# Transposes regrouped in the expert blocks, a relu shared with VectorE in 64-token blocks, and the first transposes of a fused attention + MoE kernel cut into parts

## The chip, the cores and the metric

The kernel runs on one core of one Trainium2 chip. The metric is the time of one execution on the device in microseconds (us), as the median of several executions. Three executions of the kernel before gave 520.6, 523.1 and 522.89 us: a median of 522.89. A profile comes from one further execution. Its engines are called PE (TensorE; PEld is its loading of the stationary operand), DVE (VectorE), ACT (ScalarE), POOL (GpSimd) and SP (SyncE, which here issues most DMAs).

## The reference

Sigmoid attention over 8 batches of 12 heads, 448 tokens and 64 dimensions; its rows are then tokens of a top-1 mixture of 8 experts, with a skip gate:

```python
scores = scale * np.matmul(q, k.transpose(0, 1, 3, 2)) - np.log(S)
attn = 1.0 / (1.0 + np.exp(-scores))
x = np.matmul(attn, v)                      # then reshaped to (3584, 768)
do_compute = x @ w_skip > 0
xc = x[do_compute]
e_idx = np.argmax(xc @ w_gate, axis=1)      # gate_w: its softmax weight
for e in range(8):
    mask = e_idx == e
    h = np.maximum(xc[mask] @ w1[e], 0.0)   # 768 -> 1024
    y[mask] = gate_w[mask, None] * (h @ w2[e])
out[do_compute] = xc + y
```

All inputs and outputs are float32.

## The kernel before

**Attention.** 48 steps, each a pair of heads of one batch. A step has four chunks `c` of keys. `prep` (L186) turns k and q of the pair with one VectorE block transpose each into a tile `x` whose partitions are the dimensions; `scores` (L197) makes a chunk's scores with four matmuls of 64x64 by 448 (224 in the last chunk); `weigh` (L227) takes the sigmoid on ACT; `values` (L231) multiplies by v, two chunks later, into `pa`; `keep_values` (L667) moves the result out of `pa` with one ACT copy (L668) and one VectorE add (L247). Before the first step, `keep_busy(10)` (L626) issues ten matmuls of the identity with itself; the first pair's k and q come in four small DMAs and are completed by copies on POOL and ACT (L607 to L609); the two transposes of the first pair are L627 and L628. All engines work through their instructions in the order in which this code is written (`tc.manual_schedule()`).

**Two blocks with the first expert.** After the last step, rows `x0` of 256 tokens, fetched by two gathers (L707), go through `turn_x` (L486: three 128x128 transposes on PE per half), `split_x` (L501: each float32 operand becomes a rounded part `xh` made by ACT, L495, and a rest `xl` made by DVE, L499), `gemm1` and `gemm2`. Their PSUM banks are those that attention's `pa` tiles had: three in a pool `ps_t` (through `new_t`) and one in `ps_b`. `b0_px0` and `b0_px1`, the turned rows of the first block, come from `new_t`; the one bank of `ps_b` is next used for the second half of the first block's hidden layer (`new_ph`, L799).

**The loop over the other blocks** (L1537). Each round picks one of four arms by a table that the kernel has made. In this run's order: one SPLIT, a HALF, a FULL, a HALF, then four times FULL and FEW, then a last FULL and FEW.

- FULL and SPLIT (`block`, L1323) work on 128 tokens: `gemm1(h)` makes half h of the hidden layer as 18 matmuls of 128x512 each, `relu` (ACT, L522), `turn_h(h)` (L524: four transposes into `pht[h]`), `split_h(h)` (L531: ACT makes `hh`, DVE makes `hl`), and `gemm2(j)` for j = 0..7, six matmuls of 128x384 each; j below 4 needs half 0, the others half 1. In between, the rows of the *next* block, `xn`, are turned into `pxt` (`turn_x`), after which `fetch` (L1266) lets POOL gather the rows of the block after that into `xn`, and `ready_x` (L1095) makes `xh`, `xf` (ACT) and `xl` (DVE) from `pxt`. SPLIT also splits the next expert's weights: the last statement of its arm (L1378) has DVE compute five rests of 128x768, `lo2(3)` to `lo2(7)` (L1224), after the block's own results are out.
- HALF (`half`, L1451) works on 64 tokens, with unsplit weights: two sides of 512 hidden columns land side by side in one PSUM bank, `ph[0]`; ACT applies relu in three pieces into `hs` (L1472); PE turns `xn` (6 transposes) and then `hs` (4 transposes, L1480) into the banks `pht[0]` and `ph[1]`; ACT copies them out in two pieces of 256 columns (L1486); then 32 matmuls make `py`. Its first instructions on DVE are the two of `take_rec` (L1315), which copy the block's record.
- FEW (`few`, L1382) does the same for 32 tokens.

Within an arm each engine follows the written order, and from round to round each engine passes from one arm straight to the next. The lines that set the order in HALF:

```python
for s in (slice(0, P), slice(P, 2 * P), parts[1]):
    nc.scalar.activation(hs[:, s], ph[0][:, s], AF.Relu)
...
for h in range(2):
    turn_x(xn, h, pxt[h])
fetch()
for c in range(4):
    nc.tensor.transpose(turned[c // 2][...], hs[:, c * P : (c + 1) * P], ident)
for s, p in zip(parts, turned):
    nc.scalar.activation(ht[:, s], p[:, : 2 * P], AF.Copy)
```

Of the kernel before, what the change touches and what calls it, by code (L numbers as in the profile page):

```python
# [10 lines left out]
F32 = mybir.dt.float32  # L11
# [3 lines left out]
AF = mybir.ActivationFunctionType  # L15
ALU = mybir.AluOpType
# [3 lines left out]
P = 128  # L20
# [3 lines left out]
def kernel(  # L24
# [11 lines left out]
    nc = tc.nc  # L36

    B, H, S, D = q.shape
# [4 lines left out]
    BT = 32  # L43
    NR7 = S // D
# [5 lines left out]
    NK2 = FF // P  # L50
# [23 lines left out]
    ident = const.tile([P, P], F32, name="ident")  # L74
# [43 lines left out]
    wk = att.enter_context(tc.tile_pool(name="wk", bufs=2))  # L118
# [8 lines left out]
    def new_s(name):  # L127

        turn[0] ^= 1
        return ps_s.tile([P, 2, 512], F32, tag=f"s{turn[0]}", name=name)  # L130
# [55 lines left out]
    def prep(b, hp, t, xs=None):  # L186

        n = 0 if xs is None else 1
        if xs is None:
            xs = wk.tile([P, 2, S], F32, tag="b0", name=f"x_{b}_{hp}")  # L190
        nc.vector.transpose(  # L191
            xs[:, n].rearrange("p (r j) -> p j r", j=NJ),
            t.rearrange("p (j d) -> p j d", d=D)[:, :, :BT],
        )
        return xs

    def scores(b, hp, c, xs):  # L197

        if (b, hp, c) == (0, 0, 2):
            sc = ps_a.tile([P, 2, 512], F32, tag="a", name="s_third")
        else:
            sc = new_s(f"s_{b}_{hp}_{c}")
        for m in range(2):
            first, qs = (4 * m + c, slice(0, S)) if c < 3 else (3, slice(m * HQ, (m + 1) * HQ))
            for j in range(2):
                r = slice(j * D, (j + 1) * D)
                nc.tensor.matmul(  # L209
                    sc[m * D : (m + 1) * D, j, : qs.stop - qs.start],  # L210
                    xs[r, 0, first::NR7],
                    xs[r, 1, qs],
                    start=True,
                    stop=True,
                )
        return sc
# [4 lines left out]
    def new_t(name):  # L221

        if ps_t is None:
            return new_s(name)[:, 0, :]
        return ps_t.tile([P, 512], F32, tag="t", name=name)
# [257 lines left out]
        nc.gpsimd.tensor_tensor(lo, r, hi, op=ALU.subtract)  # L483


    def turn_x(x, h, px):  # L486
        for j in range(3):
            i = 3 * h + j
            nc.tensor.transpose(  # L489
                px[:, j * P : (j + 1) * P], x[:, i * P : (i + 1) * P], ident  # L490
            )
# [29 lines left out]
    def relu(h, hs, ph):  # L521
        nc.scalar.activation(hs[:, h * H1 : (h + 1) * H1], ph[h], AF.Relu)  # L522

    def turn_h(h, hs, pt):  # L524
        for j in range(4):
            m = 4 * h + j
            nc.tensor.transpose(  # L527
                pt[:, j * P : (j + 1) * P], hs[:, m * P : (m + 1) * P], ident
            )
# [5 lines left out]
    def gemm2(j, hh, hl, py):  # L535
        h, m = divmod(j, 4)
        js = slice(m * P, (m + 1) * P)
        parts = [(n, o) for n in range(3) for o in range(2)]
        for n, o in parts:
            a, w = ((hh, wh2), (hh, wl2), (hl, wh2))[n]  # L540
            last = nc.tensor.matmul(  # L541
                half_y(py, o),
                a[h][:, js],
                w[j][:, o * H2 : (o + 1) * H2],
                start=(j == 0 and n == 0),
                stop=(j == NK2 - 1 and n == 2),
            )
        return last
# [33 lines left out]
    steps = [(b, hp) for b in range(B) for hp in range(NPAIR)]  # L582
# [33 lines left out]
    def part(n):  # L616
        return [kq[n // 2][:, j, n % 2] if n else kq0[:, j, 0] for j in range(2)]
# [4 lines left out]
    def keep_busy(n):  # L622
        for _ in range(n):
            nc.tensor.matmul(idle[:, 0, :P], ident, ident, start=True, stop=True)

    keep_busy(10)  # L626
    xs = prep(*steps[0], part(0)[0])  # L627
    xs = prep(*steps[0], part(0)[1], xs)  # L628
    ramp = const.tile([P, NX], F32, name="ramp")
    nc.vector.memset(ramp[:, NE:NX], 0.0)  # L630
    nc.vector.tensor_copy(ramp[:, :NE], ramp_i)
# [39 lines left out]
    for n, (b, hp) in enumerate(steps):  # L671
# [39 lines left out]
        for c in range(4):  # L711
            at = wk.tile([P, 2, S], F32, tag="A", name=f"at_{b}_{hp}_{c}", bufs=5)
            sc = scores(b, hp, c, xs)
# [71 lines left out]
        xs = xs_next  # L785
# [33 lines left out]
    for _ in range(2):  # L819
# [8 lines left out]
    ps_b = ctx.enter_context(  # L828
        tc.tile_pool(name="ps_b", bufs=1, space=bass.MemoryType.PSUM, reuse_waits="tile")
    )  # L830
    for h in range(2):
        px = new_t(f"b0_px{h}")
        turn_x(x0[0], h, px)
        split_x(h, px, xh0, xl0)
    logits(pl, [NK1 - 1], xt, 4)
# [2 lines left out]
    ph = new_ph(0)  # L838
    py = new_s("b0_py")
# [483 lines left out]
    def block(i, last):  # L1323


        def split1(js, h):
            if last:
                for j in js:
                    hi1(j, h)
                for j in js:  # L1330
                    lo1(j, h)

        look_ahead(ds(i + 3, 1))
        gemm1(0, range(G1), xh, xl, ph, last)
        relu(0, hs, ph)
        split1(range(3), 0)
        gemm1(1, range(9), xh, xl, ph, last)
        turn_h(0, hs, pht[0])
        split_h(0, pht[0], hh, hl)
        take_rec()  # L1340
        split1(range(3, NK1), 0)
        gemm1(1, range(9, G1), xh, xl, ph, last)
        relu(1, hs, ph)
        for h in range(2):
            turn_x(xn, h, pxt[h])
        fetch()
        split1(range(3), 1)
        gemm2(0, hh, hl, py)
        turn_h(1, hs, pht[1])
        split_h(1, pht[1], hh, hl)  # L1350
        split1(range(3, NK1), 1)
        if last:
            for h in range(2):
                whole_x(h, (slice(0, 3),))
        else:
            ready_x()
        next_rec(i)
        for j in range(1, NK2):
            gemm2(j, hh, hl, py)
        if last:  # L1360
            for j in range(2):
                hi2(j)
            for h in range(2):
                hi_x(h, pxt[h], xh)
            for j in range(2, NK2 - 2):
                hi2(j)
            for j in range(3):
                lo2(j)
            for j in range(NK2 - 2, NK2):
                dve.tensor_copy(wh2[j], raw2[j])  # L1370
            for h in range(2):
                lo_x(h, pxt[h], xh, xl)
        for o in range(2):
            rows = ys if last else yt
            weigh_sum(rows[:, o * H2 : (o + 1) * H2], half_y(py, o), recs[:, 0, 0:1])
        put(P, last)
        advance(1 if last else 2)
        if last:  # L1378
            for j in range(3, NK2):
                lo2(j)  # L1380
# [70 lines left out]
    def half(i):  # L1451

        nx = named()
        take_rec()

        def side(dst, g, n, a, w, j, most):
            nc.tensor.matmul(  # L1457
                dst[g * MD : (g + 1) * MD, :n],
                a,
                w,  # L1460
                start=(j == 0),
                stop=(j == most - 1),
                tile_position=(0, g * MD),
            )

        for j in range(NK1):
            for h in range(2):
                side(ph[0], h, H1, xf[:, j, :], raw1[j][h], j, NK1)
        turned = (pht[0], ph[1])
        parts = [slice(0, 2 * P), slice(2 * P, 4 * P)]  # L1470
        for s in (slice(0, P), slice(P, 2 * P), parts[1]):
            nc.scalar.activation(hs[:, s], ph[0][:, s], AF.Relu)  # L1472
        for h in range(2):
            for g in range(2):
                load_w1(g, h, nx)
        for h in range(2):
            turn_x(xn, h, pxt[h])
        fetch()
        for c in range(4):
            nc.tensor.transpose(  # L1480
                turned[c // 2][:, (c % 2) * P : (c % 2 + 1) * P],
                hs[:, c * P : (c + 1) * P],
                ident,
            )
        for s, p in zip(parts, turned):
            nc.scalar.activation(ht[:, s], p[:, : 2 * P], AF.Copy)  # L1486
        ready_x()

        ht8 = ht.rearrange("p (c h t) -> p c h t", c=4, h=2)
        for n in range(NK2):  # L1490
            c, h = divmod(n, 2)
            m = h * (NK2 // 2) + c
            for o in range(2):
                side(
                    py[1],
                    o,
                    H2,
                    ht8[:, c, h, :],
                    raw2[m][:, o * H2 : (o + 1) * H2],
                    n,  # L1500
                    NK2,
                )
        for g in range(3):
            load_w2(g, nx)
        look_ahead(ds(i + 3, 1))
        for o in range(2):
            s = slice(o * H2, (o + 1) * H2)
            weigh_sum(ys[:MD, s], py[1][o * MD : (o + 1) * MD, :H2], recs[:MD, 0, 0:1])
        next_rec(i)
        put(MD)  # L1510
        advance()
# [58 lines left out]
```

## Time and profile before

| what | value |
|---|---|
| median of 3 executions | 522.89 us (520.6 to 523.1) |
| the profiled execution: its time | 523.23 us |
| its span, from first to last instruction | 521.5 us |
| mean granted PE clock in it | 0.994 |
| attention | 0 to about 283 us |
| two blocks with the first expert | about 283 to 325 us |
| the loop's blocks | about 325 to 521.5 us |

The profiled execution took 1.7 us more than its span. A row of the timeline or of the chain of waits gives a start and a duration, both in us, then the engine, the line, the operation, output<-input and a count; in brackets stands how long the engine had been idle and what ended that. The chain of waits is followed back from the last instruction, at each step to what released it or, if nothing did, to the instruction before it on its engine. Rows of line groups give busy us and the mean ns of one.

### The profile page before, as it was taken

The page shows a single profiled execution, that of the slowest core. Times are in us where ns is not written, and L with a number is a line of the kernel's source. Part 1 is how long each engine was busy: PE and PEld are TensorE (multiplying, and loading weights), DVE is VectorE, ACT ScalarE, POOL GpSimd, SP SyncE. Part 2 cuts the span into 40 slices and gives each one's busy share as a digit, 9 for nine tenths or more (in the row PEclk, how much of TensorE's full clock was granted, in tenths as well). Part 3 has the DMA queues.
Part 4 walks back from the last instruction along what each step waited for, and adds up shares of the span by engine and source line. Part 5 has one row for each costly group of instructions (what it writes and reads, how often), then busy time and mean ns, then how long its engine had stood idle before and what let it go on. Part 6 is the DMA issues. An engine that isn't in the chain of part 4 may idle for free.

```text
span 521.5 us, 15403 instructions
## 1 busy us (share of the span) xinstructions
PE 506.7 (97%) x5031; PEld 343.2 (66%) x5032; DVE 292.4 (56%) x692; ACT 278.8 (53%) x481; POOL 239.5 (46%) x355
## 2 busy tenths in 40 slices
PE   8999999999999999999999999999999999999991
PEld 6885554555555555555445889857769797979790
DVE  3545766667668677776684872582221322349522
ACT  4776786766767866677666212661122323258321
POOL 3523454353556767665775401332331334444534
PEclk9999999999999999999999999999999999999997
DMA  8999977897999999999975105949395878797943
GB/s 206 201 233 194 198 159 153 178 178 171 197 195 239 216 194 205 215 193 224 199 158 111 26 31 163 386 131 356 116 339 214 251 300 283 269 328 234 346 185 47
DMA packets 142081, 107.22 MB, mean 206 GB/s; under 512 B 99163, under 2 KB 114523, under 8 KB 142032
## 3 DMA queue, kind: packets, MB, share of 16 engines
q1 hardware_dynamic: 133792, 96.11, 71.1%
q0 software_dynamic: 4032, 8.51, 6.8%
q10 hardware_dynamic: 4208, 1.95, 1.5%
q8 instruction: 30, 0.49, 0.4%
q14 instruction: 19, 0.16, 0.1%
HBM read 98.49 MB, written 17.56 MB: 223 GB/s over the span
## 4 chain that ended last, share of the span: by engine, by line
PE 91%; DMA 2%; DVE 2%; ACT 1%; issue 1%; POOL 1%; SPq 1%; ACTq 0%; POOLq 0%; DVEq 0%
PE s L209 24%; PE pa L237 23%; PE ph L513 11%; PE py L541 11%; PE b_ph L513 3%; PE b_py L541 3%; PE ph L1388 2%; PE py L1388 2%; PE py L1457 2%; PE ph L1457 2%; PE pxt L489 2%; PE pl L277 1%; PE pht L527 1%; DMA out_dram<-ys,rp 1%; PE pg L294 1%
## 5 line engine op out<-in xcount | busy, mean ns | idle before, releaser
L229 ACT ACTIVATE at<-s,bias 128x896 f32<-128x896 f32 (+1 forms) x191 | 173.5, 914 | 83.0 <-PE s L209 72.3
L209 PE MATMUL s<-x 64*64 64x448 f32 (+1 forms) x1528 | 172.3, 497 | 2.1 <-DVE sel L404 0.8
L237 PE MATMUL pa<-at,v 64*64 64x448 f32 (+1 forms) x1536 | 170.3, 489 | 0.0
L173 POOL COPY kq<-kq 32x896 f32<-32x896 f32 (+1 forms) x96 | 87.5, 912 | 97.6 <-DMA kq<-in_q_dram 48.7
L209 PEld LDWEIGHTS s<-x 64*64 64x64 f32 x1528 | 84.7, 191 | 51.2 <-issue 27.0
L237 PEld LDWEIGHTS pa<-at,v 64*64 64x64 f32 x1536 | 68.3, 133 | 54.1 <-issue 45.6
L191 DVE STREAM_TRANSPOSE x<-kq 128x448 f32<-128x448 f32 x94 | 80.7, 933 | 5.3 <-POOL kq L173 5.3
L247 DVE TENSOR_TENSOR xt<-xt,pa 128x448 f32<-128x448 f32 x48 | 29.8, 620 | 53.0 <-ACT xt L668 53.0
L411 POOL DMA_INDIRECT lst<-rec,idx x32 | 31.8, 995 | 16.7 <-issue 5.3
L483 POOL TENSOR_TENSOR wl<-wr,wh 128x384 fp32r<-128x384 f32 (+1 forms) x28 | 31.2, 1127 | 11.4 <-DVE wh L482 6.9
L252 DVE STREAM_TRANSPOSE y<-xt 128x448 f32<-128x448 f32 x48 | 31.0, 645 | 8.9 <-DMA out_dram<-y 7.4
L533 DVE TENSOR_TENSOR hl<-pht,hh 128x512 fp32r<-128x512 f32 x14 | 9.7, 690 | 41.8 <-ACT hh L532 35.1
L522 ACT ACTIVATE hs<-ph 128x512 f32<-128x512 f32 x14 | 8.4, 599 | 42.1 <-PE ph L513 26.2
L571 POOL DMA_INDIRECT out_dram<-ys,rp x15 | 22.8, 1520 | 16.2 <-POOLq L1537 8.4
L541 PE MATMUL py<-wh,hh 128*128 128x384 f32 x112 | 29.8, 347 | 0.0
L541 PE MATMUL py<-wh,hl 128*128 128x384 f32 x112 | 28.8, 338 | 0.0
L541 PE MATMUL py<-wl,hh 128*128 128x384 f32 x112 | 28.7, 337 | 0.0
L499 DVE TENSOR_TENSOR xl<-pxt,xh 128x384 fp32r<-128x384 f32 x30 | 15.3, 552 | 20.9 <-ACT xf L1087 20.2
L513 PE MATMUL ph<-wl,xh 128*128 128x512 f32 x84 | 26.3, 400 | 0.0
L668 ACT ACTIVATE xt<-pa 128x448 f32<-128x448 f32 x48 | 25.7, 536 | 0.8 <-PE pa L237 0.8
L513 PE MATMUL ph<-wh,xh 128*128 128x512 f32 x84 | 25.4, 399 | 0.0
L513 PE MATMUL ph<-wh,xl 128*128 128x512 f32 x84 | 24.1, 391 | 0.0
(263 smaller groups left out, 650.7 us busy)
## 6 DMA issues: line engine op xcount, KB each, us to landing
raw<-in_moe_w_dram SPq DMA_DIRECT2D x48, 768.0 KB
v<-in_v_dram SPq DMA_DIRECT2D x48, 256.0 KB
out_dram<-y SPq DMA_DIRECT2D x192, 56.0 KB
raw<-in_moe_w_dram SPq DMA_DIRECT2D x7, 1536.0 KB
kq<-in_k_dram SPq DMA_DIRECT2D x46, 224.0 KB
kq<-in_q_dram SPq DMA_DIRECT2D x46, 224.0 KB
wr<-in_moe_w_dram SPq DMA_DIRECT2D x12, 256.0 KB
wr<-in_moe_w_dram SPq DMA_DIRECT2D x16, 192.0 KB
```

The costliest lines, as they stand in the source:

```text
L173: nc.gpsimd.tensor_copy(a[BT:, :, :, :BT], a[:BT, :, :, BT:])
L191: nc.vector.transpose(xs[:, n].rearrange("p (r j) -> p j r", j=NJ), t.rearrange("p (j d) -> p j d", d=D)[:, :, :BT],)
L209: nc.tensor.matmul(sc[m * D : (m + 1) * D, j, : qs.stop - qs.start], xs[r, 0, first::NR7], xs[r, 1, qs], start=True, stop=True,)
L229: nc.scalar.activation(at[:, :, :n], sc[:, :, :n], AF.Sigmoid, bias=bias, scale=SCALE)
L237: nc.tensor.matmul(pa[j * D : (j + 1) * D, r, qs], vt[rs, j, r + c if c < 3 else 3 * (1 - r), :], at[rs, j, : qs.stop - qs.start], start=( ...
L247: nc.vector.tensor_tensor(x, x, pa[:, 1, :S], op=ALU.add)
L252: nc.vector.transpose(y, xts[b][:, hp, :])
L411: put = nc.gpsimd.indirect_dma_start(out=lst[:, :], out_offset=bass.IndirectOffsetOnAxis(ap=idx[:, c : c + 1], axis=0), in_=rec[:, c, :], ...
L483: nc.gpsimd.tensor_tensor(lo, r, hi, op=ALU.subtract)
L513: nc.tensor.matmul(ph[h], a[:, j * P : (j + 1) * P], w[j][h], start=(n == 0), stop=(n == len(t) - 1),)
L541: last = nc.tensor.matmul(half_y(py, o), a[h][:, js], w[j][:, o * H2 : (o + 1) * H2], start=(j == 0 and n == 0), stop=(j == NK2 - 1 and n ...
L668: nc.scalar.activation(xts[b][:, hp, :], pa[:, 0, :S], AF.Copy)
```

## The change

Four places. In HALF the second relu piece goes to VectorE, the last two pieces stay one ACT instruction, the first two pieces of `hs` are turned ahead of the last transpose of `xn`, and the copies out of PSUM are four of 128 columns. In `block`, `turn_x(xn)` and `fetch` go from before `gemm2(0)` to behind `turn_h(1)`, which itself now follows `gemm2(1)`. For the first pair, k is turned in four parts by chunk and q in two halves, between k's second and third part; the first chunk's scores are made by halves of the queries, and there are nine `keep_busy` matmuls instead of ten. `b0_px0` lies in `ps_b`'s bank.

```diff
@@ scores @@
+        if (b, hp, c) == (0, 0, 0):
+            by_u = [t.rearrange("p s (r u n) -> p s u r n", r=BT, u=2) for t in (xs, sc[:, :, :S])]
+            for u in range(2):
+                for m in range(2):
+                    for j in range(2):
+                        r = slice(j * D, (j + 1) * D)
+                        nc.tensor.matmul(
+                            by_u[1][m * D : (m + 1) * D, j, u],
+                            xs[r, 0, 4 * m :: NR7],
+                            by_u[0][r, 1, u],
+                            start=True,
+                            stop=True,
+                        )
+            return sc
@@ before the first step @@
-    keep_busy(10)
-    xs = prep(*steps[0], part(0)[0])
-    xs = prep(*steps[0], part(0)[1], xs)
+    keep_busy(9)
+    xs = wk.tile([P, 2, S], F32, tag="b0", name="x_first")
+    xv = xs.rearrange("p s (r u n) -> p s u n r", r=BT, u=2)
+    kv, qv = (t.rearrange("p (u n d) -> p u n d", u=2, d=D)[:, :, :, :BT] for t in part(0))
+    for c in range(4):
+        cs = slice(c, c + 5, 4) if c < 3 else slice(3, 4)
+        nc.vector.transpose(xv[:, 0, :, cs], kv[:, :, cs])
+        if c == 1:
+            for u in range(2):
+                nc.vector.transpose(xv[:, 1, u], qv[:, u])
@@ first block with the first expert @@
-        px = new_t(f"b0_px{h}")
+        px = new_t("b0_px1") if h else ps_b.tile([P, 512], F32, tag="b", name="b0_px0")
@@ block @@
         relu(1, hs, ph)
+        split1(range(3), 1)
+        for j in range(2):
+            gemm2(j, hh, hl, py)
+        turn_h(1, hs, pht[1])
         for h in range(2):
             turn_x(xn, h, pxt[h])
         fetch()
-        split1(range(3), 1)
-        gemm2(0, hh, hl, py)
-        turn_h(1, hs, pht[1])
         split_h(1, pht[1], hh, hl)
...
-        for j in range(1, NK2):
+        for j in range(2, NK2):
             gemm2(j, hh, hl, py)
@@ half @@
-        parts = [slice(0, 2 * P), slice(2 * P, 4 * P)]
-        for s in (slice(0, P), slice(P, 2 * P), parts[1]):
-            nc.scalar.activation(hs[:, s], ph[0][:, s], AF.Relu)
+        parts = [slice(c * P, (c + 1) * P) for c in range(4)]
+        nc.scalar.activation(hs[:, parts[0]], ph[0][:, parts[0]], AF.Relu)
+        nc.vector.tensor_scalar(hs[:, parts[1]], ph[0][:, parts[1]], 0.0, None, op0=ALU.max)
+        nc.scalar.activation(hs[:, 2 * P : 4 * P], ph[0][:, 2 * P : 4 * P], AF.Relu)
...
-        for h in range(2):
-            turn_x(xn, h, pxt[h])
+        def turned_h(cs):
+            for c in cs:
+                nc.tensor.transpose(turned[c // 2][:, parts[c % 2]], hs[:, parts[c]], ident)
+
+        turn_x(xn, 0, pxt[0])
+        turn_x(xn, 1, pxt[1], range(2))
+        turned_h(range(2))
+        turn_x(xn, 1, pxt[1], range(2, 3))
         fetch()
-        for c in range(4):
-            nc.tensor.transpose(
...
-        for s, p in zip(parts, turned):
-            nc.scalar.activation(ht[:, s], p[:, : 2 * P], AF.Copy)
+        turned_h(range(2, 4))
+        for c, s in enumerate(parts):
+            nc.scalar.activation(ht[:, s], turned[c // 2][:, parts[c % 2]], AF.Copy)
```

(`turn_x` gets a fourth argument, the transposes to do.) Where the change moves instructions, three places of the program, with the change's own line numbers in its rows. First PE in HALF, from the last matmuls into `ph` to the first into `py`; before:

```order
L489 MATMUL pxt<-ident,xn 128x128 x6
L1480 REGISTER_ALU
L1480 MATMUL pht<-ident,hs 128x128
L1480 REGISTER_ALU
L1480 MATMUL pht<-ident,hs 128x128
L1480 REGISTER_ALU
L1480 MATMUL ph_4385<-ident,hs 128x128 x2
L1457 ISA
L1457 MATMUL py_4387<-raw_0_4380,ht 64x384 x2
```

and of the change:

```order
L503 MATMUL pxt<-ident,xn 128x128 x5
L1502 REGISTER_ALU
L1502 MATMUL pht<-ident,hs 128x128
L1502 REGISTER_ALU
L1502 MATMUL pht<-ident,hs 128x128
L503 MATMUL pxt<-ident,xn 128x128
L1502 REGISTER_ALU
L1502 MATMUL ph_4392<-ident,hs 128x128 x2
L1479 REGISTER_ALU
L1479 MATMUL py_4394<-raw_0_4387,ht 64x384 x2
```

The second transpose of `hs`, which reads VectorE's piece, now stands ahead of the sixth of `xn`. Second, DVE and ACT around that relu, of the change, with the semaphores each row waits for. On DVE, the end of SPLIT's arm is five `wl` rows of L1245, and HALF's arm begins:

```order
L1338 COPY recs<-rn 128x2 [waits DMAHW0_I-4477_own,DVE_I-4477_own,DMAHW4_I-4477_own,DMAHW1_49]
L1339 REGISTER_ALU
L1339 CAST rid<-recs 128x1 [waits Pool_I-4477_own,DVE_I-4477_own,DMASW3_49,DVE_49]
L1494 REGISTER_ALU
L1494 TENSOR_SCALAR hs<-ph_4391 128x128 [waits Activation_I-4477_own]
L513 ISA
```

and on ACT the three pieces' rows and the copies stand as:

```order
L1493 ACTIVATE hs<-ph_4391 128x128 [waits PE_I-4477_own,Activation_I-4477_own,DVE_I-4477_own,Activation_49]
L1495 REGISTER_ALU
L1495 ACTIVATE hs<-ph_4391 128x256 [waits DVE_I-4477_own]
L1511 REGISTER_ALU
L1511 ACTIVATE ht<-pht 128x128 [waits PE_I-4477_own]
L1511 REGISTER_ALU
L1511 ACTIVATE ht<-pht 128x128 [waits Activation_I-4477_own]
```

VectorE's piece is the third instruction of DVE's arm; it waits on ACT (the first piece), and ACT's third piece waits on DVE: the three pieces, all read from the one bank `ph[0]`, are held one behind the other. Third, PE in FULL from the end of `gemm1(1)`; before:

```order
L489 MATMUL pxt<-ident,xn 128x128 x6
L541 ISA
L541 MATMUL py_4386<-wh_0_113,hh_4364 128x384
L541 REGISTER_ALU
L541 MATMUL py_4387<-wh_0_113,hh_4364 128x384
L541 MATMUL py_4386<-wl_0_121,hh_4364 128x384
L541 MATMUL py_4387<-wl_0_121,hh_4364 128x384
L541 REGISTER_ALU
L541 MATMUL py_4386<-wh_0_113,hl_4367 128x384
L541 MATMUL py_4387<-wh_0_113,hl_4367 128x384
L527 REGISTER_ALU
L527 MATMUL pht<-ident,hs 128x128 x4
```

and of the change, from the second half of `gemm2(0)` on:

```order
L555 MATMUL py_4393<-wh_0_113,hl_4374 128x384
L555 MATMUL py_4394<-wh_0_113,hl_4374 128x384
L555 MATMUL py_4393<-wh_1_114,hh_4371 128x384
L555 MATMUL py_4394<-wh_1_114,hh_4371 128x384
L555 MATMUL py_4393<-wl_1_122,hh_4371 128x384
L555 MATMUL py_4394<-wl_1_122,hh_4371 128x384
L555 MATMUL py_4393<-wh_1_114,hl_4374 128x384
L555 MATMUL py_4394<-wh_1_114,hl_4374 128x384
L541 REGISTER_ALU
L541 MATMUL pht<-ident,hs 128x128 x4
L503 MATMUL pxt<-ident,xn 128x128 x6
```

The ten transposes stand together behind twelve `py` matmuls, where before six of them stood ahead of the first `py` matmul and four behind the sixth.

More of the change, by code (lines that the diff above doesn't have):

```diff
@@ L483, in wsplit, with turn_x @@
         nc.gpsimd.tensor_tensor(lo, r, hi, op=ALU.subtract)
-    def turn_x(x, h, px):
-        for j in range(3):
+    def turn_x(x, h, px, js=range(3)):
+        for j in js:
             i = 3 * h + j
@@ L1475, in half @@
                 load_w1(g, h, nx)
-        for h in range(2):
-            turn_x(xn, h, pxt[h])
-        fetch()
-        for c in range(4):
[L1480 to L1484, printed above, removed]
-        for s, p in zip(parts, turned):
-            nc.scalar.activation(ht[:, s], p[:, : 2 * P], AF.Copy)
+        def turned_h(cs):
[5 more added lines that the diff above has]
+        turn_x(xn, 1, pxt[1], range(2, 3))
+        fetch()
+        turned_h(range(2, 4))
+        for c, s in enumerate(parts):
+            nc.scalar.activation(ht[:, s], turned[c // 2][:, parts[c % 2]], AF.Copy)
         ready_x()
```

## The prediction, made before the change was run

> **What bounds the kernel now.** I read the page first (span, busy shares, the shares of the chain of waits):
>
> ```profile
> span 521.5 us, 15403 instructions
> PE 506.7 (97%) x5031; PEld 343.2 (66%) x5032; DVE 292.4 (56%) x692; ACT 278.8 (53%) x481; POOL 239.5 (46%) x355
> PE 91%; DMA 2%; DVE 2%; ACT 1%; issue 1%; POOL 1%; SPq 1%; ACTq 0%; POOLq 0%; DVEq 0%
> ```
>
> PE is busy for 97% of the span and carries 91% of the chain. So only two things count: how long PE's own work takes, and the few places where it waits. What another engine gains or loses counts where PE waits for it. The chain of waits through the two HALF blocks and the FULL behind them (start, us, what) shows which places those are:
>
> ```profile
> 343.13 5.30 PE ph L1457 x24
> 348.43 0.81 PE pxt L489 x6
> 349.23 0.23 PE pht L1480 x2
> 349.47 0.02 issue
> 349.49 0.39 ACT ht L1486
> 349.88 0.09 issue
> 349.97 5.38 PE py L1457 x32
> ...
> 380.13 0.39 ACT ht L1486
> 380.53 0.09 issue
> 380.62 5.38 PE py L1457 x32
> ...
> 394.88 0.66 PE pxt L489 x6
> 395.53 1.05 PE py L541 x6
> 396.58 0.44 PE pht L527 x4
> 397.02 7.37 PE py L541 x42
> 404.39 2.76 PE ph L1388 x96
> 407.15 0.26 PE pht L1409
> 407.40 0.66 PE pxt L489 x6
> ```
>
> A HALF leaves the chain to ACT for about 0.5 us: PE has turned half of `hs` and waits for the first copy `ht` (0.39 + 0.09). In FULL and FEW the chain stays on PE. The sum therefore has five terms. It is made on the profiled execution, 523.23 us, which is 0.34 above the median of 522.89.
>
> **The first HALF: +2.4 us.** The second relu piece is now VectorE's. What VectorE is doing at that time, what ACT did then, and two groups of lines (busy us, mean ns) for the price of the new pieces:
>
> ```profile
> 346.64 4.43 DVE L1224 TENSOR_TENSOR wl<-raw,wh 128x768 fp32r<-128x768 f32 x5
> 350.99 0.16 DVE L1317 COPY recs<-rn 128x2 f32<-128x2 f32 x1
> 351.06 0.15 DVE L1318 CAST rid<-recs 128x1 int32<-128x1 f32 x1
> ...
> 348.58 0.72 ACT L1472 ACTIVATE hs<-ph 128x128 f32<-128x128 f32 x3 [3.92 <-PE ph L1457]
> ...
> L1321 DVE TENSOR_SCALAR yt<-py,recs 128x384 f32<-128x384 f32 x10 | 5.7, 613 | 20.1 <-PE py L541 20.1
> ...
> L1472 ACT ACTIVATE hs<-ph 128x128 f32<-128x128 f32 x4 | 0.9, 275 | 14.5 <-PE ph L1457 14.5
> ```
>
> VectorE goes from SPLIT's arm straight into HALF's. The five rests that end SPLIT's arm run from 346.64 to 351.07, back to back, with HALF's two record copies behind them until 351.21. The relu is the third instruction of HALF's arm. ACT's first piece ends near 348.9 (348.58 and 0.275), and then the bank's readers stand still for VectorE until 351.21. Nothing in the change lets VectorE start the rests earlier.
>
> From there, step by step:
> - VectorE's piece, 128x128. No row has it. By VectorE's own rows it lies between a copy of one column (0.15) and 128x384 out of PSUM (0.61); on the line between these it is 0.15 + 0.46/3 = 0.30. Ready at 351.5.
> - ACT's last piece, 128x256, stands behind VectorE's piece in the order of the change. With 0.1 for the hand-over (the 0.09 "issue" of the chain) and 0.39 (the chain's `ht` copy has the same 256 columns): ready at 352.0.
> - PE's transposes 2 and 3 of `hs`. `ht`'s first copy needs only PE's first two, but it is ACT's next instruction after the 256 columns, so it starts at about 352.0 and takes some 0.28.
> - `py` begins at 352.0 + 0.28 + 0.1, about 352.4, where it began at 349.97: **+2.4 us**. Bounds: +2.1, if ACT's last piece needs no wait for VectorE's (then only PE's transpose 1 and the copy behind it are late); +2.8, if the piece and its two hand-overs cost as the 0.61 row does.
>
> Queued behind the waiting pieces: on ACT the copies `ht`, then `xh` and `xf` for the next block; on PE the sixth transpose of `xn` and with it POOL's gather; on VectorE nothing that had been earlier. The next block's first matmul shifts with `py`, so these keep their distance.
>
> A rule that speaks against a gain here, in sentences that the sum doesn't need: the Trainium skill, page "PSUM — Partial Sum Buffer", section "PSUM bank collisions raise a hardware error", says that two engines must be kept off the same bank and partitions at the same time, two readers too, whatever the columns. No row of before shows ACT and VectorE at one bank together. By that rule the pieces stay one behind the other and the HALF costs +2.4; without it, +2.1.
>
> **The second HALF: +0.2 us.** Here VectorE has nothing to finish:
>
> ```profile
> 377.53 0.15 DVE L1318 CAST rid<-recs 128x1 int32<-128x1 f32 x1
> ...
> 379.23 0.72 ACT L1472 ACTIVATE hs<-ph 128x128 f32<-128x128 f32 x3 [10.62 <-PE ph L1457]
> ```
>
> VectorE is through with the records at 377.68, 1.55 before the relu. The three pieces in turn: ACT 379.23 to 379.5; hand-over, VectorE 379.6 to 379.9; hand-over, ACT 380.0 to 380.4; then the first copy `ht`, 0.28, to 380.7; `py` at 380.8 against 380.62. What is won by a smaller first copy (0.39 less 0.28) and by two transposes moved ahead is lost on two hand-overs. Bounds: −0.33, if VectorE's and ACT's last piece run beside each other (ACT's relu done at 379.9, two hundredths for the turn, copy and start at 380.29), and +0.5, if VectorE's piece takes 0.6.
>
> **The regrouped transposes in FULL and SPLIT: 0.** In the chain above the six `pxt` transposes take 0.66 and the four `pht` 0.44, both 0.11 each, and the `py` matmuls take 0.175 in the run of 6 (1.05) as in the run of 42 (7.37). A group has no start price in these rows, so one group less saves nothing: between 0 and −0.1 over 7 blocks (the hundredth to which the rows are rounded). What moves is cover:
>
> ```profile
> 397.19 0.60 ACT L532 ACTIVATE hh<-pht 128x512 fp32r<-128x512 f32 x1 [1.60 <-PE py L541]
> ...
> 397.83 0.69 DVE L533 TENSOR_TENSOR hl<-pht,hh 128x512 fp32r<-128x512 f32 x1 [3.45 <-issue]
> 399.29 1.02 DVE L499 TENSOR_TENSOR xl<-pxt,xh 128x384 fp32r<-128x384 f32 x2 [0.77 <-ACT xf L1087]
> ...
> 396.77 1.05 POOL L561 DMA_INDIRECT xn<-out_dram,rp  x1 [0.72 <-PE pht L527]
> ...
> DMA to landing us min/median/max: 3.9/5.7/6.8
> ```
>
> (The last line is the answer for gathers into `xn` over all of the loop.) `turn_h(1)` now begins 2.10 after `gemm1` (12 matmuls) instead of 1.71, and `hh` and `hl` end at most 0.4 to 1.0 later, by 399.5. Their first reader, `gemm2(4)`, comes after the ten transposes and 24 matmuls: 394.88 + 1.10 + 4.20 = 400.2, as before. `xl` ends by 401.3 and is wanted at 404.39. The gather is issued about 2.2 later, near 399.0, and lands by 399.0 + 6.8 = 405.8; its transposes in FEW stand at 407.40. All covers hold, the thinnest (the gather) by 1.6 us.
>
> **`b0_px0` in `ps_b`'s bank: −0.3 us.**
>
> ```profile
> 280.08 1.07 POOL L561 DMA_INDIRECT x<-out_dram,rp  x1 [1.43 <-issue]
> ...
> 284.43 0.62 DVE L247 TENSOR_TENSOR xt<-xt,pa 128x448 f32<-128x448 f32 x1
> 285.10 0.87 PE L489 MATMUL b_px<-ident,x 128*128 128x128 f32 x6 [0.24 <-DVE xt L247]
> 285.73 0.87 ACT L495 ACTIVATE b<-b_px 128x384 fp32r<-128x384 f32 x2 [1.34 <-PE b_px L489]
> ...
> DMA to landing us min/median/max: 4.5/4.7/4.8
> ```
>
> The transposes waited for VectorE's add on the bank that they take over (284.43 + 0.62 = 285.05). In `ps_b`'s bank, which ACT left long before, the first three wait only for the rows: 280.08 + 4.5 to 4.8 gives 284.6 to 284.9, against 285.10. The other three still wait for the add. ACT's `xh`, on which `gemm1` waits, comes some 0.3 sooner. Bounds −0.4 (rows already there when PE has issued its logits) and 0 (landing last, or the logits behind them take it back).
>
> **The first pair: 0.**
>
> ```profile
> 4.59 1.72 DVE L191 STREAM_TRANSPOSE x<-kq_first 128x448 f32<-128x448 f32 x2 [3.16 <-ACT kq_first L608]
> ...
> 9.75 0.14 PEld L237 LDWEIGHTS pa<-at,v 64*64 64x64 f32 x2 [0.77 <-DMA v<-in_v_dram]
> ```
>
> Scores could start when half of q is turned, up to 0.43 sooner (half of q's share of the 1.72). But PE then comes to `values` of the first chunk and waits for a load of v, until 9.75, which the change doesn't move. What is won ahead is waited there, a wait that was already 0.77. Bounds −0.43 (v's load was later by chance in this execution) and +0.3 (six VectorE instructions instead of two, with a fixed part of 0.15 each as in the `rid` row, less what overlaps).
>
> **The sum.** 523.23 + 2.4 + 0.2 − 0.3 + 0 + 0 = 525.5 for an execution like the profiled one, and 522.89 + 2.3 = **525.2** as a median. What a measurement of this kernel can tell from no change is about 0.5%, 2.6 us: from 520.3 to 525.5. The forecast lies just inside.
>
> **The rivals.**
> - *VectorE helps in both HALFs.* It would need to come to the relu before the rests, or the rests to end sooner. Then each HALF wins 0.33 and with the bank's 0.3 the median is 522.89 − 0.96 = 521.9. Against it stand the rests' rows and the order on DVE, which puts `lo2` ahead. A form of this is that the change does not do what it says, with VectorE's piece free anyway: 0.10.
> - *Slower by more, since the gather of `xn` comes late in FEW.* Place: the transposes at 407.40. It decides from 8.4 us after an issue at 399.0; then the slowest landing of 6.8 has become longer, as other loads now run beside it. With 9.5 us each of five FEW blocks waits 1.1: 525.2 + 5.5 = 530.7. No landing in before is near 8.4: 0.06.
> - *Slower by more, since PE's clock falls after the 2 us in the first HALF.* Place: `py` at 352.4, 5.38 us long, which at half clock would take 5.38 more: 530.6. PE's waits in before reach 0.77 and the mean granted clock is 0.994, so no row shows what follows 2 us: 0.03. The Trainium skill, page "TensorE: Matmul & The Clock Gate", section "Why this matters for your kernels", advises against PE gaps of more than about 3 us; a gap of 2 us stays below that.
> - *The head wins.* If the v load comes sooner in most executions, its 0.43 shows, and 525.2 becomes 524.8; with the HALF at its lower bounds (+2.1 and −0.33) 523.9 to 524.0. This stays mostly within the forecast's range: 0.08 for what lies under 524.0.
>
> **How the numbers follow.** The forecast's own range is 524.0 to 526.5 (terms between the bounds, and some tenths for executions) with 0.73; help in both HALFs 0.10 at 521.9; the head and the lower bounds 0.08, from 522.6 to 524.0; the two slower rivals 0.09 near 530. For 8 in 10 the range goes from 522.6 to 526.8. Faster than 520.3 would need more than every gain at its bound together (−0.66, −0.4, −0.43, −0.1) and more, out of the first rival's share: 0.03. Slower than 525.5: the rivals' 0.09 and somewhat over a third of the forecast's 0.73, 0.36 in all. Within: 0.61.
>
> **What would show it.** In the profile after, the row of VectorE's relu in the first HALF begins behind `rid`, at 351.2, and not near 348.9; PE shows an idle of about 2 us ahead of a transpose of `hs`, ended by DVE; in the second HALF the three pieces stand one behind the other and `py` begins within 0.5 of where it did; in FULL no new wait ahead of `gemm2(4)`, and in FEW none ahead of `pxt`; `b_px` is released by a DMA; PE's wait for v is still there, longer by what scores win. The prediction is wrong if VectorE runs the relu before the rests, if ACT's and VectorE's pieces overlap, or if a row of transposes ahead of `gemm2` turns out to cost more than 0.11 each.

## The result, and the profile after

The changed kernel takes 529.13 us (median of 6, 525.64 to 530.72), the kernel before 523.0 us (median of 6, 520.6 to 524.61): a ratio of 1.0119, 95% interval 1.0086 to 1.0151. The forecast was 525.2 us with a range of 522.6 to 526.8. The sign was right, the size and the place were not.

The profiled execution took 529.19 us. Its page, span and shares as before:

```profile
span 527.1 us, 15408 instructions
PE 508.8 (97%) x5037; PEld 347.5 (66%) x5038; DVE 294.9 (56%) x698; ACT 279.5 (53%) x483; POOL 236.7 (45%) x355
PE 94%; DVE 2%; issue 1%; DMA 1%; POOL 1%; ACT 0%; ACTq 0%; DVEq 0%; POOLq 0%
```

PE is still the bound, but one view has two rows that the kernel before lacks, what PE waited for (engine and line, what ended the wait: us in total, times, longest):

```profile
PE ph L1410 <- DVE ys L1342: 2.5, 1, 2.5
PE ph L1479 <- DVE ys L1342: 2.5, 1, 2.5
```

L1479 is the first matmul of a HALF, L1410 that of a FEW. Both come right behind a SPLIT. (The run has two SPLITs, the first block of the loop and the one from 460.86 in the trace of before; the text above counts the second as a FULL, which is an error.) The chain of waits from the first SPLIT to the FULL and FEW behind the second HALF:

```profile
333.68 5.98 PE py L555 x34
...
340.65 1.02 DVE xl L513 x2
341.67 0.54 DVE ys L1342
342.20 0.24 issue
342.44 7.16 PE ph L1479 x24
349.61 0.70 PE pxt L503 x5
350.30 0.48 PE pht L1502 x2
...
350.96 0.41 PE ph L1502 x2
351.37 5.31 PE py L1479 x32
356.68 6.37 PE ph L527 x27
...
375.07 5.30 PE ph L1479 x24
380.37 0.70 PE pxt L503 x5
381.07 0.52 PE pht L1502 x2
...
381.77 0.41 PE ph L1502 x2
382.18 5.31 PE py L1479 x32
387.49 6.35 PE ph L527 x27
...
405.86 2.76 PE ph L1410 x96
408.62 0.26 PE pht L1431
408.88 0.66 PE pxt L503 x6
```

PE's last `py` matmul of the SPLIT ends at 339.99. Then PE stands until 342.44, when VectorE has made the first half of `ys`. In before, the same matmul began when `py` ended (343.13), 2.2 us ahead of the start of `ys`, whose row there is:

```profile
345.30 1.13 DVE L1321 TENSOR_SCALAR ys<-py,recs 128x384 f32<-128x384 f32 x2
```

And then, in the change, the 24 `ph` matmuls take 7.16 us, where the second HALF's, and both of before, take 5.30. The windows view (us of the window; busy us and count of each engine; granted PE clock, DMA share, GB/s) shows why:

```profile
core 0: us, PE busy (x) PEld busy (x) DVE busy (x) ACT busy (x) POOL busy (x), PEclk, DMA share, GB/s
339.90:342.40 2.50, 0.09 (x1) 0.00 (x0) 2.50 (x6) 1.05 (x2) 0.00 (x0) 1.00 0.00 0
342.40:345.80 3.40, 3.35 (x10) 1.96 (x12) 3.37 (x7) 0.00 (x0) 2.00 (x2) 0.63 0.00 0
...
343.50:344.00 0.50, 0.50 (x4) 0.30 (x2) 0.50 (x2) 0.00 (x0) 0.42 (x1) 0.50 0.00 0
...
345.80:349.60 3.80, 3.80 (x17) 1.86 (x14) 1.69 (x4) 0.00 (x0) 0.00 (x0) 0.88 0.91 154
...
480.80:483.10 2.30, 0.00 (x0) 0.00 (x0) 2.30 (x6) 0.85 (x2) 0.00 (x0) 1.00 0.00 0
483.10:486.50 3.40, 3.35 (x65) 3.35 (x69) 3.37 (x7) 0.28 (x1) 1.97 (x2) 0.52 0.22 18
```

Behind the 2.45 us without work the windows of 3.4 us show a mean clock of 0.63, and of 0.52 behind the second SPLIT, where FEW's 96 `ph` matmuls take 4.49 us in place of 2.76. These are means of two values: the trace's record of the granted clock has 0.50 from 343.30 to 346.72 and from 483.25 to 486.66, and 1.00 before and after. Half of the clock for 3.41 us is 1.7 us of lost work, near the 1.86 and 1.73 that the two stretches lose. And here are VectorE and ACT in the first HALF (timeline: start, us, engine, line):

```profile
347.35 0.15 DVE L1339 CAST rid<-recs 128x1 int32<-128x1 f32 x1
350.11 0.29 DVE L1494 TENSOR_SCALAR hs<-ph 128x128 f32<-128x128 f32 x1 [2.62 <-ACT hs L1493]
...
349.80 0.28 ACT L1493 ACTIVATE hs<-ph 128x128 f32<-128x128 f32 x1 [8.86 <-PE ph L1479]
350.44 0.38 ACT L1495 ACTIVATE hs<-ph 128x256 f32<-128x256 f32 x1 [0.35 <-DVE hs L1494]
```

VectorE was not late for its relu: it had been free since 347.50 and waited for ACT. PE had been held up by 2.45 us of waiting and 1.86 of slow matmuls, and in that time VectorE finished the five rests.

**Where 5.6 us of span come from.** From the loop's first `ph` matmul to the end of its last `py` matmul the trace of before has 186.24 us, that of the change 194.83: +8.59. By blocks (start to start): the two SPLITs 2.4 each, the HALF behind the first 2.02, the FEW behind the second 1.69, the other HALF 0.19, together 8.7, and a tenth less in the other blocks. Against that, attention ended 3.1 us sooner in this execution (the last ACT copy out of `pa` begins at 280.73, in before at 283.85). The experiments show both parts apart.

### The profile page after: what moved, and what is told of

Its sections match the earlier page's. It is cut to its first block, busy times and chain, and to the rows that moved or that the text cites. A ratio compares the mean times of both kernels' runs of the same rounds, so it can differ in the third digit from the quotient of the medians.

```text
span 527.1 us, 15408 instructions
## 1 busy us (share of the span) xinstructions
PE 508.8 (97%) x5037; PEld 347.5 (66%) x5038; DVE 294.9 (56%) x698; ACT 279.5 (53%) x483; POOL 236.7 (45%) x355
## 4 chain that ended last, share of the span: by engine, by line
PE 94%; DVE 2%; issue 1%; DMA 1%; POOL 1%; ACT 0%; ACTq 0%; DVEq 0%; POOLq 0%
PE s L223 24%; PE pa L251 24%; PE ph L527 11%; PE py L555 11%; PE b_ph L527 3%; PE b_py L555 3%; PE ph L1410 3%; PE ph L1479 2%; PE py L1410 2%; PE py L1479 2%; PE pxt L503 2%; PE pl L291 2%; PE pht L541 1%; PE pg L308 1%; DMA kq_first<-in_q_dram 1%
## 5 line engine op out<-in xcount | busy, mean ns | idle before, releaser
L223 PE MATMUL s<-x 64*64 64x448 f32 (+1 forms) x1504 | 168.6, 496 | 0.5 <-DVE sel L418 0.5
L223 PEld LDWEIGHTS s<-x 64*64 64x64 f32 x1504 | 83.5, 191 | 47.2 <-issue 23.1
```

Of the source, the lines that this page charges most:

```text
L223: nc.tensor.matmul(sc[m * D : (m + 1) * D, j, : qs.stop - qs.start], xs[r, 0, first::NR7], xs[r, 1, qs], start=True, stop=True,)
```

## What makes PE wait: the theory

The order of the two programs, with the semaphores (counters that one engine raises and another waits for) of each row, has the wait. The first `ph` matmul of a HALF, before and after:

```
L1457 MATMUL ph_4384<-raw_0_0_4362,xf 64x512 [waits Activation_I-4470_own,DMAHW3_49,DMAHW0_I-4470_own,Activation_49]
L1479 MATMUL ph_4391<-raw_0_0_4369,xf 64x512 [waits Activation_I-4477_own,DVE_I-4477_own,DMAHW3_49,DMAHW0_I-4477_own,Activation_49]
```

`DVE_..._own` is new, and the first `ph` matmuls of FULL, SPLIT and FEW have it too. In a loop whose arms are picked at run time, a block's first matmul into `ph[0]` must wait for whoever read that bank in the round before, whichever arm that was. As long as only ACT read it, that was a wait for ACT. Since HALF's relu on VectorE reads it, every arm waits for a count of VectorE's instructions in the round before. In the program that is built from the kernel each round counts 32 of them, and the wait is for the 24th: HALF's relu (HALF has 11 and counts 22 with its first). A SPLIT has 32, and its 24th is the first `ys`, which comes late because VectorE also makes the rests and casts of the next expert's weights. A FULL's 24th is `hl` of its second half and a FEW's the second of its record copies, both done well before their block ends, so only a SPLIT makes PE wait. That is theory T, with the low clock behind the wait as its second part. The rivals: the loss comes from the regrouped transposes or px0's bank (A); the matmuls behind the wait are slow because their data come late (B); PE needs `ys` itself, or a bank that it frees (C).

## The experiments

Every run is compared with the kernel before on the same chip. Beside the ratio, a table at the end has the length of the loop in one profile of each, which repeats much better than the whole time.

**e1: the relu back on ACT.**

```diff
-        nc.vector.tensor_scalar(hs[:, parts[1]], ph[0][:, parts[1]], 0.0, None, op0=ALU.max)
+        nc.scalar.activation(hs[:, parts[1]], ph[0][:, parts[1]], AF.Relu)
```

> The changed kernel with one edit: the second relu piece of HALF is ACT's again (as 128 columns), all else as changed. Theory T (what costs is that VectorE reads ph[0] in HALF: the first ph matmul of every arm then waits for VectorE's 24th step of the round before, which in a SPLIT round is the first ys; 2.45 us at each of two SPLITs, and PE's granted clock is near 0.63 for the next 4 us, +1.86 and +1.73): no wait of PE for DVE ys, both stretches behind a SPLIT at clock 1.0, so 529.1 - 8.5 = 520.6, between 519 and 523. Rival A (the loss lies in the regrouped transposes or in px0's new bank): the two waits stay and the time is 526 or more.

Measured: 520.53 us against 521.92, ratio 0.9974 (0.9958 to 0.9989). The two waits are gone, and the chain has PE alone from SPLIT to FULL:

```profile
334.23 6.32 PE py L555 x36
340.55 5.30 PE ph L1479 x24
345.85 0.69 PE pxt L503 x5
346.55 0.32 PE pht L1502 x2
346.86 0.11 PE pxt L503
346.97 0.31 PE ph L1502 x2
347.28 5.38 PE py L1479 x32
```

From the end of `ph` to the start of `py` it takes 1.43 us (before 1.54, with a wait for ACT in it). The whole loss is VectorE's relu, and the rest of the change is a small gain: A falls. This version is faster than the change and, by a quarter of a per cent, than the kernel before.

**e2: only the relu on VectorE, in the kernel before.**

```diff
-        for s in (slice(0, P), slice(P, 2 * P), parts[1]):
-            nc.scalar.activation(hs[:, s], ph[0][:, s], AF.Relu)
+        nc.scalar.activation(hs[:, :P], ph[0][:, :P], AF.Relu)
+        nc.vector.tensor_scalar(hs[:, P : 2 * P], ph[0][:, P : 2 * P], 0.0, None, op0=ALU.max)
+        nc.scalar.activation(hs[:, parts[1]], ph[0][:, parts[1]], AF.Relu)
```

> The kernel before with one edit: the second relu piece of HALF on VectorE, nothing else of the change. T: the same two waits of PE for ys appear, with the low clock behind them, 523.0 + 2 x 2.45 + 1.86 + 1.73 + two HALFs of some 0.3 = 531.5 to 532.5, more than the whole change costs. Rival A: at most the HALF's own wait, 523 to 525.5.

Measured: 529.63 us, ratio 1.0142 (1.0113 to 1.0172). Both waits for `ys` are there (2.6 and 2.3), and the `ph` matmuls behind the first take 7.18 us at a granted clock of 0.57. The loop is 8.73 longer than in before, near the expected 9; the median is 2 us below what was expected. One instruction of 0.3 us makes the loss.

**e3 and e5: PE kept busy through the wait.** At the end of SPLIT's matmuls, 20 and 10 matmuls of the identity into `pht[0]`:

```diff
         for j in range(2, NK2):
             gemm2(j, hh, hl, py)
         if last:
+            for _ in range(20):
+                nc.tensor.matmul(pht[0][:, :P], ident, ident, start=True, stop=True)
```

> The changed kernel with 20 matmuls of the identity with itself (0.11 us each, 2.2 us) into the bank pht[0] at the end of SPLIT's matmuls, where PE waits for ys. T (the stretch behind the wait is long because PE's clock falls after idle 2.45 us): the wait for ys still ends when it did, but the first ph matmuls of the next block take 5.3 (HALF) and 2.8 us (FEW) in place of 7.16 and 4.49: 529.1 - 3.6 = 525.5. Rival B (those matmuls are slow because their data, weights or xf, come late): they stay at 7.2 and 4.5 and the time is 529.

Measured: 536.25 us, ratio 1.0276 (1.0247 to 1.0306): the expectation missed, for two reasons of its own making. The 20 matmuls took 4.46 us and not 2.2 (each float32 one shows as two records of 0.11). And at the first SPLIT, PE stood for another 4.0 us behind them, to 349.13; an instruction load of 16 KB lies at 343.94 to 345.01 there and in none of the other profiles, so this place says nothing of T. At the second SPLIT, where PE went on without a gap, FEW's 96 matmuls took 2.98 us in place of 4.49.

> As e3, with half as many matmuls: ten of the identity with itself, 0.22 us each by e3's rows, 2.2 us, which end before the wait of 2.45 us does. T (low clock after an idle PE): the waits still end with the first ys, but the ph matmuls behind them take 5.3 and 2.8 us at clock 1.0 in place of 7.16 and 4.49; 529.1 - 3.6 = 525.5. Rival B (their data come late): 7.2 and 4.5 stay, 529.

Measured: 528.61 us, ratio 1.0114 (1.0096 to 1.0132). The chain at the first SPLIT, and the clock in three windows:

```profile
344.44 0.54 DVE ys L1342
344.98 0.24 issue
345.22 5.47 PE ph L1481 x24
```

```profile
342.70:345.20 2.50, 2.24 (x21) 2.06 (x20) 2.50 (x6) 1.02 (x2) 0.00 (x0) 1.00 0.00 0
345.20:350.60 5.40, 5.38 (x24) 3.00 (x24) 5.03 (x10) 0.00 (x0) 2.00 (x2) 1.00 0.38 49
...
484.20:487.90 3.70, 3.40 (x97) 2.71 (x98) 3.67 (x7) 0.28 (x1) 1.98 (x2) 1.00 0.28 74
```

The wait still ends with `ys`, but the clock stays at 1.00, and the 24 matmuls take 5.47 us where they took 7.16. B falls for the HALF. The FEW took 3.64 from start to its `pht` (4.49 in the change, 2.76 in before): half of what it lost came back, at a clock of 1.00. In it two matmuls start 0.53 apart, at 486.16 and 486.69, with PE idle for 0.26 of that; the cause isn't known. In e3 the same 96 took 2.98 without such a stop, so late data aren't needed for their 4.49 either. The loop is 2.44 shorter than the change's, not 3.6. The median hardly shows it, since attention ended at 283.43 in this profile, 2.7 later than in the change's.

**e6: the relu two steps earlier.** HALF's relu ahead of the two record copies, so that it counts as step 22:

```diff
         nx = named()
-        take_rec()
...
         nc.vector.tensor_scalar(hs[:, parts[1]], ph[0][:, parts[1]], 0.0, None, op0=ALU.max)
+        take_rec()
```

> The changed kernel with VectorE's relu ahead of the two record copies of HALF's arm, so that it is counted as step 22 in place of 24. T: a SPLIT's 22nd step is its first xl, whose end stands 1.0 us ahead of that of the first ys; PE's waits are 1.4 to 1.5 in place of 2.45, and the total 529.1 - 2 = 527, less whatever a shorter idle saves of the clock (at most 3.6: 523.5). Rival C (PE waits for ys itself): waits of 2.45, 529.

Measured: 527.03 us, ratio 1.0091 (1.0074 to 1.0108). What PE waited for, and two windows:

```profile
PE ph L1478 <- DVE xl L513: 1.5, 1, 1.5
PE ph L1410 <- DVE xl L513: 1.5, 1, 1.5
```

```profile
340.60:342.10 1.50, 0.04 (x1) 0.03 (x1) 1.50 (x4) 0.99 (x2) 0.00 (x0) 1.00 0.00 0
342.10:347.50 5.40, 5.40 (x25) 2.98 (x25) 5.37 (x10) 0.00 (x0) 2.00 (x2) 1.00 0.17 30
```

The wait now ends with `xl`, which nobody in `ph` needs, 1.0 us sooner, as the count says. C falls. Behind these two waits of 1.47 us the clock stays at 1.00. So both parts of the loss shrink, and the loop is 4.5 longer than before's, as the median is by 4.4. That the median meets the 527 that was expected with the low clock still in it is chance: the change's own median lies 2.5 below what its loop says.

**e4: the relu ten steps earlier.** Ten tiny VectorE instructions at the end of HALF's arm (and the tile `spare` that they write):

```diff
+        for k in range(10):
+            nc.vector.memset(spare[:, k : k + 1], 0.0)
         next_rec(i)
```

> The changed kernel with ten tiny VectorE instructions (a memset of one column each, to a tile that nothing reads) at the end of HALF's arm; they move VectorE's relu from the 24th to the 14th of 32 counted steps of its arm. T: PE's wait at a SPLIT's end is for step 14, long past, so both waits and the low clock behind them go (-8.5), and VectorE's relu in the first HALF, which now comes when it did before, waits for the five rests as forecast (about +2.2, and possibly a low clock behind that gap, up to +1.9): 522.8 to 524.7. Rival C (PE needs ys itself, or a bank that ys frees): the waits stay, 529.

Measured: 525.83 us, ratio 1.0072 (1.0049 to 1.0095). Ten instructions more make it 3 us faster than the change, though 1.1 above the top of what was expected. No wait for `ys` is left; and now the first HALF shows what the prediction said of it. VectorE in that HALF, and PE's waits:

```profile
343.53 4.43 DVE L1245 TENSOR_TENSOR wl<-raw,wh 128x768 fp32r<-128x768 f32 x5
347.88 0.16 DVE L1338 COPY recs<-rn 128x2 f32<-128x2 f32 x1
...
348.01 0.28 DVE L1494 TENSOR_SCALAR hs<-ph 128x128 f32<-128x128 f32 x1
```

```profile
PE pht L1502 <- DVE hs L1494: 1.6, 1, 1.6
...
PE ph L527 <- ACT yt L1464: 0.8, 1, 0.8
```

`py` begins at 349.51, 3.78 after the `ph` matmuls' end (345.73), where before has 1.54: +2.2. Its 32 matmuls then take 6.64 in place of 5.38: the clock's record has 0.50 from 348.75 to 352.17. The second wait, which was not expected, in the FULL behind the second SPLIT's FEW, ends when VectorE has made that FEW's first record copy (487.63 + 0.16, queued behind the five rests): the same kind of wait, one block further on, since a FEW's first VectorE instruction counts 23. The view names ACT's `yt` there, but in the change the same matmul began at 491.47, ahead of that `yt` (491.65), so it doesn't need it.

**e7: the first pair's part alone**, and **e8: e1 without it.** Diffs: the first two pieces of the change's diff, put into before, and taken out of e1.

> The kernel before with the first pair's part of the change alone. By the profiles of four runs with it (first copy out of pa at 16.05 to 16.49) and two without (16.43 and 17.03) it is worth between 0 and 0.5: 0.9985 of before, within the interval of 1. The rival, that the 3 us by which attention ended earlier in the changed kernel's profile come from it, gives 0.994.

Measured: 522.57 us against 522.66, ratio 1.0000 (0.9987 to 1.0013).

> The kernel of e1 (no relu on VectorE) without the first pair's part: px0's bank (-0.31 by the rows), HALF's new order on ACT (-0.11 and -0.12), the regrouped transposes (0). 522 - 0.55, a ratio of 0.999, against 0.9974 measured for e1. If it comes out as e1 does, the head is worth nothing.

Measured: 521.84 us, ratio 0.9985 (0.9971 to 0.9998); the interval touches e1's, so whether the first pair's part adds anything to e1 stays open. That attention ended sooner in the change's profile is not its doing: the last copy out of `pa` stood at 283.11 with it in e7, at 282.25 without it in e8, and anywhere from 280.6 to 283.9 in the ten profiles.

The lengths in one profile each, in us: from that last copy to the loop's first `ph` matmul, and from there to the end of the last `py`:

| kernel | ahead of the loop | the loop |
|---|---|---|
| before | 40.76 | 186.24 |
| the change | 40.85 | 194.83 |
| e1, relu on ACT | 40.47 | 186.18 |
| e2, only the relu on VectorE | 41.14 | 194.97 |
| e3, 20 matmuls in the wait | 40.85 | 200.99 |
| e4, ten steps earlier | 40.81 | 190.95 |
| e5, 10 matmuls in the wait | 40.85 | 192.39 |
| e6, two steps earlier | 40.85 | 190.74 |
| e7, only the first pair | 40.76 | 186.23 |
| e8, e1 without the first pair | 40.48 | 186.16 |

Two things can be read off. px0's bank is worth 0.28 ahead of the loop (e8 against before). And with VectorE's relu the loop begins 0.38 later (before to e2, e1 to the change): its first matmul waits for VectorE as well (e2's chain has VectorE's last instruction of the first expert's rows, 0.04, and 0.14 of issue there).

## Why the prediction was wrong

- **The step that failed** is in "The first HALF", in the paragraph on what is queued behind the waiting pieces. It looked for waits inside HALF's arm, followed those whom VectorE's piece makes late in that block, and let the next block's first matmul merely shift with `py`; a wait at the blocks' borders was put at nothing without a look at it. But `ph[0]` had got a new reader, VectorE, for whom the *next* block's first `ph` matmul must wait, in every arm and by a count that stands for something else in each. That cost 2.45 us behind each SPLIT, with 1.86 and 1.73 of slow matmuls behind the two waits; e1 takes it away and e2 alone brings it. The second SPLIT wasn't seen at all. "In FULL and FEW the chain stays on PE" is true of before and not of the change, where a FEW follows a SPLIT.
- **The first HALF's +2.4** was the right mechanism under the assumption that PE arrives when it did. In the change ACT's first piece began 6.87 us behind the start of the five rests, where before has 1.94: 2.45 of waiting and 1.86 of slow matmuls lay ahead of it, and the rests began 0.57 sooner, counted from SPLIT's last `py` matmul. (That nothing in the change lets VectorE start the rests earlier was wrong by this much.) With the count moved away, e4 measured +2.2, with the relu behind the five rests and at 0.28 us (0.30 estimated). That the size agrees so well is in part luck: counted from the end of `ph`, the relu began 0.50 sooner than forecast, and from there to `py` it took 1.50 where 1.2 was forecast, with the last two transposes at half the clock.
- **The low clock** was a rival with a chance of 0.03, priced at 5.38. It came true at another place: +1.86 and +1.73. Half the clock was right; it lasts for 3.41 us in each case and not for a whole stretch. In e4 it came at the place that the rival named, and `py` took 1.26 longer. The text said that no row of before showed what follows 2 us of idling; that was a reason for a larger chance, not a smaller one. The Trainium skill, page "TensorE: Matmul & The Clock Gate", section "Why this matters for your kernels", advises against PE gaps of more than about 3 us. Here gaps of 2.45 and of 1.60 us brought half the clock, and 1.47 us did not, so that a gap stays below 3 us was no reason to set the rival aside: the measurement decides.
- **The second HALF's +0.2**: 1.81 from the end of `ph` to `py` against 1.55, +0.26. The three pieces stand one behind the other as forecast; a hand-over took 0.03 where 0.1 was assumed (in the first HALF's rows, 350.08 to 350.11 and 350.40 to 350.44), and `py` waited a little longer for PE's own transposes.
- **px0's −0.3** was right (−0.28), **the regrouped transposes' 0** too: the FULL ahead of the first FEW takes 18.37 (387.49 to 405.86) where it took 18.39, and `pxt` in FEW waits for no gather. The gather itself was issued 2.5 later in its block, not 2.2: 12 `py` matmuls and the four `pht` now stand ahead of the six `pxt`. **The first pair's 0** was right in e7.
- What stays open: medians show +6.1 (4.5 to 7.9) for the change where its loop shows +8.6. Attention's spread of 3 us from one profile to the next covers the difference, but what sets that spread wasn't tried. The same holds for e1, whose median gains 1.4 where the table's two lengths gain 0.35.

## What to carry to other kernels

When an operation moves to another engine, list what it reads and writes, and look up who touches those tiles next, in every arm that can follow: in a loop with arms picked at run time a new reader of a shared bank is a wait for all of them, and how late it ends is decided by the arm that ran in the round before, not by the one that was edited. A comparison of the waits of each block's *first* instruction on the bounding engine, before and after, would have shown it. And a wait of 2.5 us cost TensorE another 1.7 to 1.9 us of low clock.

## What was not expected of the hardware

- With each idle stretch of PE of 2.45 us (the change, twice), 2.64 and 2.31 (e2), 3.98 (e3) and 1.60 (e4) the granted clock fell to 0.50 for 3.41 us, beginning between 0.3 us before PE took up work again and 0.9 us after; with the two of 1.47 us (e6) it stayed at 1.00. In e5, where matmuls of no use left stops of only 0.28 and 0.22, the clock stayed at 1.00.
- The clock's changes lie on a grid. In the change it was 1.00 for 337.92 us, 0.50 for 3.41, 1.00 for 136.53, 0.50 for 3.41 and 1.00 for 34.13: 99, 1, 40, 1 and 10 times 3.413. So what a gap costs may depend on where it falls on this grid, and no run here moved one gap along it.
- In e3 PE did nothing for 4.0 us (345.15 to 349.13) behind an instruction load of 16 KB that ended at 345.01, in a spot where no other profile has one. That the load is the cause was not shown, nor that the added matmuls brought it there.
